# The second parts of the split weights, made on TensorE in PSUM instead of on VectorE

## The chip, the cores and the metric

The kernel runs on one core of a Trainium2 chip. The metric is the device time of one execution in microseconds (us). The engines are TensorE (PE in the profile, its weight loads PEld), VectorE (DVE), ScalarE (ACT), GpSimd (POOL) and SyncE (SP, which issues the DMAs). Each engine works through its own queue in the order in which the program has it, and waits for the others by semaphores.

## What is computed

Attention with a threshold, followed by an expert layer without a gate:

```python
scores = scale * np.matmul(q, k.transpose(0, 1, 3, 2))      # q, k, v: 8 x 8 x 576 x 64
thresh = np.max(scores, axis=-1, keepdims=True) - tau
scores = np.where(scores >= thresh, scores, -1000000000.0)
attn = softmax(scores)
x = (attn @ v), heads side by side                            # 4608 x 512
h = x @ w_in                                                  # 512 x 2048
g = h * (1.0 / (1.0 + np.exp(-h)))
out = g @ w_out                                               # 2048 x 512
```

All of it is float32, to float32's accuracy.

## The kernel before

**Precision.** The matrix products run on f16 operands in two parts: a first part that holds the leading bits of a scaled value, and a second part that holds what is left. A product then takes three f16 matmuls (first times first, first times second, second times first). The weights are split so as well: with a power-of-two scale `sc`, the first part is `sc*w` rounded to f16, and the second is `sc*w` minus the first part.

**Weights.** They come as 32 chunks of 128 x 512 numbers, 16 of `w_in` and 16 of `w_out`, as words of float64. `load_weights` (L157) issues the DMA of a chunk, 512 KB, into one of two staging buffers (eight chunks of `w_in` go to a free part of `gbuf`). `decode_weights` (L172) rebuilds the float32: a GpSimd product (L179), a VectorE shift (L183), a VectorE combination (L186, the last reader of the low words), four small matmuls on TensorE for the chunk's largest value (L197), a sign by ScalarE (L204) and a GpSimd product with it (L205). When 16 chunks are decoded, a scale is worked out, and `split_weights` (L207) makes the two parts of each chunk: the first on ScalarE (L211), the second on VectorE (L212). The decoded chunk `i` lies in slot `i+2` of `wst`, and the two f16 parts of chunk `i` take slot `i`, so that the parts of chunk `i+2` overwrite the decoded chunk `i`.

**Attention.** The work goes in tiles of 128 queries by 576 keys, in the text softmax tiles. A tile is: scores by TensorE (L412, four matmuls for a tile of one head; the first 16 tiles use float32 operands directly, L400), a maximum on VectorE (L422), an exponential on ScalarE (L432), the mask and the sum on VectorE (L441), a product with the reciprocal on ScalarE (L454), the two f16 parts on GpSimd (L465, L468, L471; L463 on ScalarE for the first few), a transposing DMA (L481), and the product with v on TensorE (L496). The first 16 tiles transpose on TensorE instead (L357, L359) and copy out on ScalarE (L367, L368). Keys are split on ScalarE and GpSimd (L324, L326), queries on ScalarE with VectorE or GpSimd.

**Expert layer.** For a column range of x, 16 units of the first layer (`h_unit`, 12 matmuls each, L539) are followed by ScalarE and VectorE work (L547, L548, L554, L555), and 16 units of the second (`o_unit`, 12 matmuls, L570) by a copy and a store (L580, L582). The first range of batch 0 has 256 columns, the second 320; later ranges have 288.

**PSUM.** `bank` (L78) hands out a tile in one of two banks of the pool `ps_m`, in turns: to the transposes of the first 16 tiles, to the sums over partitions for scales, and to the first-layer units. A third bank, used for the decodes' matmuls, joins the turns and serves the second layer later on.

**What sets the order.** The program is written out tile by tile: in slot `t` of the main loop the operations of `todo[t]` are called, then expert units by a running credit. `W_PLAN` places loads, decodes and splits in slots (`w_in`: decodes from slot 0, splits from 13 to 22; `w_out`: decodes from 9, splits from 26, with a priority offset of 150). A scheduler then orders the instructions of each engine by priority and by its own model of when operands and buffers come free, so that a small edit can move instructions far away.

Of the kernel before, what the change touches and what calls it, by code (L numbers as in the profile page):

```python
# [9 lines left out]
F16 = mybir.dt.float16  # L10
BF16 = mybir.dt.bfloat16
F32 = mybir.dt.float32
F32R = mybir.dt.float32r
I32 = mybir.dt.int32
AF = mybir.ActivationFunctionType
ALU = mybir.AluOpType
# [3 lines left out]
P = 128  # L20
# [3 lines left out]
NK = DM // P  # L24
# [28 lines left out]
def attention_moe(  # L53
# [10 lines left out]
    nc = tc.nc  # L64
    const = ctx.enter_context(tc.tile_pool(name="const", bufs=1))
# [12 lines left out]
    def bank(shape, name, own=None):  # L78
        if own is None:
            own = turn[0] = (turn[0] + 1) % turn[1]  # L80
        return ps_m.tile(shape, F32, tag=f"m{own}", name=name)
# [7 lines left out]
        out=gate, in0=tau_sb, scalar1=0.0, scalar2=0.125, op0=ALU.is_ge, op1=ALU.mult  # L89
# [3 lines left out]
        out=ntau, in0=tau_sb, scalar1=0.0, scalar2=-1.0, op0=ALU.max, op1=ALU.mult  # L93
# [51 lines left out]
    w16 = wst.bitcast(F16)  # L145
# [2 lines left out]
    nc.vector.memset(ones, 1.0)  # L148
    ident = const.tile([P, P], F32, name="ident")
    make_identity(nc, ident)  # L150
    wsc = {}

    w_words = (w_in.bitcast(I32), w_out.bitcast(I32))
    wraw = {}
# [52 lines left out]
    def split_weights(i):  # L207
        w = wst[:, i + WSPARE, :]
        hi = w16[:, i, 0:512]
        sc = wsc["in" if i < 4 * NK else "out"][:, 0:1]  # L210
        nc.scalar.activation(hi, w, AF.Copy, scale=sc)  # L211
        nc.vector.scalar_tensor_tensor(  # L212
            out=w16[:, i, 512:1024], in0=w, scalar=sc, in1=hi, op0=ALU.mult, op1=ALU.subtract
        )

    def wi(c, f, lo):
        col = f * P
# [402 lines left out]
    start = {}  # L620
# [66 lines left out]
    for first, t0, t1, t2, hp in W_PLAN:  # L687
        for i in range(16):
            ti = t0 + i * (t1 - t0) / 16
            at(math.floor(ti - 2), pri(hp, lambda i=i + first: load_weights(i)))  # L690
            at(math.floor(ti), pri(hp, lambda i=i + first: decode_weights(i)))
        at(t1, pri(hp, scale_out if first else scale_in))
        for i in range(16):
            at(t1 + i * (t2 - t1) // 16, pri(hp, lambda i=i + first: split_weights(i)))
# [27 lines left out]
    while t < NT + 8 or units or ready or held:  # L722
# [32 lines left out]
        for v, p, c0, n in avs.pop(t, []):  # L755
# [6 lines left out]
            scale = xscale if v in direct else 2.0**-12  # L762
# [52 lines left out]
```

## Time and profile before

| | |
|---|---|
| median of three runs | 1244.9 us (1243.98 to 1248.05) |
| the profiled execution, its own time | 1244.94 us |
| its span from first to last instruction | 1243.2 us |
| PE busy | 1140.7 us, 92% of the span |
| DVE busy | 961.3 us, 77% |
| ACT busy | 818.0 us, 66% |
| POOL busy | 759.4 us, 61% |

The profile is one execution. A row of a group of instructions names the line of the kernel, the engine, the operation, what it writes and reads, the shape, the count, the busy time in us, the mean duration of one in ns, and the idle time of the engine ahead of them with what ended it. The shares of the whole span are averages over stages with different limits; the weights' decodes and splits lie in the first 190 us, and from 1000 us on mostly the expert layer is left. Busy time of PE is worked out from pipelined matmuls, whose modelled durations overlap.

### The profile page before, as it was taken

The numbers are of one execution on the slowest core, as the hardware profiler recorded it, in microseconds if no ns is written. First come the engines' busy times: TensorE is split into PE (matmuls) and PEld (weight loads), VectorE is DVE, ScalarE is ACT, GpSimd is POOL, SyncE is SP. The second block draws the span as 40 slices with busy tenths as digits, with TensorE's granted clock in tenths as the row PEclk, the third lists the DMA queues.
The fourth block names the chain that finished last, engine by engine and source line by source line (L and its number), as shares of the span: only waits on it lengthen the run. The fifth ranks groups of instructions, "written<-read, shape, count | busy, mean of one in ns | idle before, by whom it ended". The sixth has DMA issues, their size and how long they took to land.

```text
span 1243.2 us, 26997 instructions
## 1 busy us (share of the span) xinstructions
PE 1140.7 (92%) x9400; PEld 897.4 (72%) x9400; DVE 961.3 (77%) x2627; ACT 818.0 (66%) x1505; POOL 759.4 (61%) x952
## 2 busy tenths in 40 slices
PE   5674879899799989999999999999999999999998
PEld 3453657676577767777888877787777877777777
DVE  7999998978888888989888957988689848333230
ACT  5787777766777667777777747776577847433331
POOL 4568988577778768786878708773688538200000
PEclk8996889899899999999999999999999999999999
DMA  9457867678868868888778638783687436200000
GB/s 297 127 177 179 186 130 146 132 151 167 151 130 145 166 133 147 148 158 172 143 140 152 137 90 154 143 148 101 110 168 148 87 73 116 54 15 16 12 14 24
DMA packets 363480, 158.15 MB, mean 127 GB/s; under 512 B 329552, under 2 KB 338256, under 8 KB 363344
## 3 DMA queue, kind: packets, MB, share of 16 engines
q1 hardware_dynamic: 363344, 156.43, 61.9%
q8 instruction: 74, 1.21, 0.4%
q14 instruction: 62, 0.51, 0.1%
HBM read 66.72 MB, written 9.44 MB: 61 GB/s over the span
## 4 chain that ended last, share of the span: by engine, by line
PE 54%; DVE 25%; DMA 6%; ACT 6%; issue 5%; POOL 4%; SPq 0%; ACTq 0%; POOLq 0%; DVEq 0%
PE o L570 20%; PE h L539 19%; PE s L412 7%; PE a L496 7%; DVE w L441 6%; DVE sm L422 5%; DMA vraw<-in_vL 3%; DVE qstack L316 3%; ACT w L432 2%; DMA wT<-hl 2%; DVE wst L212 2%; DVE h L548 1%; DVE gbuf L555 1%; ACT w L454 1%; DVE wst L186 1%
## 5 line engine op out<-in xcount | busy, mean ns | idle before, releaser
L539 PE MATMUL h<-x,wst 128*128 128x288 f16 (+2 forms) x3072 | 430.8, 290 | 12.7 <-DVE gbuf L555 10.2
L570 PE MATMUL o<-gbuf,wst 128*128 128x288 f16 (+2 forms) x3072 | 420.6, 287 | 8.2 <-ACT wst L580 6.5
L539 PEld LDWEIGHTS <-wst 128*128 128x128 f16 x3072 | 294.6, 99 | 102.0 <-issue 22.0
L570 PEld LDWEIGHTS <-wst 128*128 128x128 f16 x3072 | 293.2, 98 | 90.5 <-issue 11.4
L468 POOL TENSOR_TENSOR hl<-w,hl 128x512 f16<-128x512 f32 x272 | 329.3, 1211 | 14.5 <-ACT hl L463 2.1
L465 POOL TENSOR_SCALAR hl<-w 128x576 f16<-128x576 f32 x264 | 180.6, 687 | 190.8 <-ACT w L454 128.3
L432 ACT ACTIVATE w<-s,sm 128x576 f32<-128x576 f32 x288 | 210.5, 738 | 83.5 <-DVE sm L422 30.6
L441 DVE SCALAR_TENSOR_TENSOR w<-s,sm,w 128x576 f32<-128x576 f32 x288 | 232.0, 812 | 32.5 <-ACT w L432 30.2
L454 ACT ACTIVATE w<-w,sm 128x576 f32<-128x576 f32 x288 | 217.6, 770 | 52.4 <-DVE sm L449 49.3
L422 DVE TENSOR_REDUCE sm<-s 128x1 f32<-128x576 f32 x288 | 215.0, 749 | 31.9 <-PE s L412 28.2
L548 DVE SCALAR_TENSOR_TENSOR h<-th,h 128x288 f32<-128x288 f32 (+2 forms) x256 | 116.2, 455 | 108.5 <-ACT th L547 106.4
L547 ACT ACTIVATE th<-h,msc 128x288 f32<-128x288 f32 (+2 forms) x256 | 126.2, 497 | 106.0 <-PE h L539 104.7
L412 PE MATMUL s<-khi,qstack 128*128 128x288 f32 x608 | 158.7, 343 | 19.0 <-DVE w L441 14.5
L554 ACT ACTIVATE gbuf<-h 128x288 f16<-128x288 f32 (+2 forms) x256 | 103.5, 407 | 81.3 <-DVE h L548 80.2
L555 DVE SCALAR_TENSOR_TENSOR gbuf<-h,gbuf 128x288 f16<-128x288 f32 (+2 forms) x256 | 114.9, 451 | 40.4 <-ACT gbuf L554 39.6
L496 PE MATMUL a<-wT,v 128*64 128x288 f16 (+1 forms) x1680 | 131.3, 298 | 13.5 <-DMA wT<-hl 13.3
L412 PE MATMUL s<-klo,qstack 128*128 128x288 f32 x608 | 132.6, 300 | 0.0
L326 POOL TENSOR_TENSOR klo<-kraw,khi 128x576 fp32r<-128x576 f32 x64 | 95.2, 1487 | 56.5 <-ACT khi L324 53.8
L412 PEld LDWEIGHTS s<-khi,qstack 128*128 128x128 f32 x608 | 97.9, 196 | 41.9 <-issue 22.9
L496 PEld LDWEIGHTS <-v 128*64 128x64 f16 x1680 | 94.5, 113 | 40.1 <-issue 30.3
L412 PEld LDWEIGHTS s<-klo,qstack 128*128 128x128 f32 x608 | 100.3, 194 | 0.3
L471 POOL TENSOR_TENSOR hl<-w,hl 128x64 f16<-128x64 f32 x272 | 100.2, 368 | 0.0
(84 smaller groups left out, 866.5 us busy)
## 6 DMA issues: line engine op xcount, KB each, us to landing
qraw<-in_qT SPq DMA_DIRECT2D x128, 144.0 KB, 3.0
kraw<-in_kT SPq DMA_DIRECT2D x128, 144.0 KB, 3.0
vraw<-in_vL SPq DMA_DIRECT2D x32, 320.0 KB, 3.7
wraw<-in_w_out SPq DMA_DIRECT2D x16, 512.0 KB, 3.8
out_t<-wst SPq DMA_DIRECT2D x56, 144.0 KB, 2.2
wT<-hl SPq DMA_TRANSPOSE x304, 3.4
gbuf<-in_w_in SPq DMA_DIRECT2D x8, 512.0 KB, 7.5
wraw<-in_w_in SPq DMA_DIRECT2D x8, 512.0 KB, 6.0
```

The costliest lines, as they stand in the source:

```text
L412: nc.tensor.matmul(s_ps[:, j, :HALF], lhs, kk[:, j * HALF : (j + 1) * HALF], start=(n == 0), stop=(n == len(seq) - 1),)
L422: nc.vector.tensor_reduce(out=negm, in_=s_ps[:, :, :HALF], op=ALU.max, axis=AX.XY, negate=True)
L432: nc.scalar.activation(wtile[t].rearrange("p (j c) -> p j c", j=2), sps[t][:, :, :HALF], AF.Exp, bias=small[t][:, 0:1],)
L441: nc.vector.scalar_tensor_tensor(out=w3, in0=s_ps[:, :, :HALF], scalar=sm[:, 1:2], in1=w3, op0=ALU.is_ge, op1=ALU.mult, accum_out=sm[:, 2:3],)
L454: nc.scalar.activation(w, w, AF.Copy, scale=r)
L465: nc.gpsimd.tensor_scalar(out=fl[:, 0:S], in0=w, scalar1=1.0, scalar2=1.0, op0=ALU.mult, op1=ALU.mult)
L468: nc.gpsimd.tensor_tensor(out=fl[:, 640:1152], in0=w[:, 0:512], in1=fl[:, 0:512], op=ALU.subtract)
L496: nc.tensor.matmul(a_ps[odd * D : (odd + 1) * D, :n], vt[:, lo_v, odd, kv, :], wT[v, b * H + 2 * p + odd][:, kw, c0 - base : c0 - base + n ...
L539: nc.tensor.matmul(ph[:, :n], wi(c, f, lo_w), x16[b, lo_x][:, c, c0 : c0 + n], start=(k == 0), stop=(k == 11),)
L548: nc.vector.scalar_tensor_tensor(out=ph[:, :n], in0=th[:, :n], scalar=1.0, in1=ph[:, :n], op0=ALU.add, op1=ALU.mult,)
L555: nc.vector.scalar_tensor_tensor(out=g[:, 1, :n], in0=ph[:, :n], scalar=2.0**-14, in1=g[:, 0, :n], op0=ALU.mult, op1=ALU.subtract,)
L570: nc.tensor.matmul(ps[:, :n], wo(f, d, lo_w), g[:, lo_g, :n], start=(f == 0 and k == 0), stop=(f == NF - 1 and k == 2),)
```

## The change

`split_weights` no longer makes the second part on VectorE. For each of the two matrices ScalarE writes a float32 diagonal `wdiag` that holds the scale; once, it writes an f16 identity with the sign turned, `minus`. For each chunk TensorE adds two products in a PSUM bank taken by `bank`: `wdiag` times the decoded chunk (float32, 512 columns), and `minus` times the first part (f16, 512 columns). ScalarE copies the bank to the place of the second part.

```diff
+    minus = const.tile([P, P], F16, name="minus")
+    nc.scalar.activation(minus, ident, AF.Copy, scale=-1.0)
     wsc = {}
+    wdiag = {}
...
     def split_weights(i):
         w = wst[:, i + WSPARE, :]
         hi = w16[:, i, 0:512]
-        sc = wsc["in" if i < 4 * NK else "out"][:, 0:1]
+        which = "in" if i < 4 * NK else "out"
+        sc = wsc[which][:, 0:1]
+        if which not in wdiag:
+            wdiag[which] = const.tile([P, P], F32, name=f"wdiag_{which}", tag="wdiag")
+            nc.scalar.activation(wdiag[which], ident, AF.Copy, scale=sc)
         nc.scalar.activation(hi, w, AF.Copy, scale=sc)
-        nc.vector.scalar_tensor_tensor(
-            out=w16[:, i, 512:1024], in0=w, scalar=sc, in1=hi, op0=ALU.mult, op1=ALU.subtract
-        )
+        rest = bank([P, 512], f"wlo_{i}")
+        nc.tensor.matmul(rest, wdiag[which], w, start=True, stop=False)
+        nc.tensor.matmul(rest, minus, hi, start=False, stop=True)
+        nc.scalar.activation(w16[:, i, 512:1024], rest, AF.Copy)
```

The lines behind it move down by three (in the first part) and by eight (behind `split_weights`): L412 of before is L420 after, L432 is L440, and the new lines are L220 and L221 (the two matmuls) and L222 (the copy).

The change also moves instructions on every engine. On the queue of SP, the loads of `w_out` (`wraw`) are mixed before with the loads of keys and queries (`kraw`, `qraw`) and with the transposes of the softmax tiles (`wT<-hl`):

```order
L169 DMA wraw_709<-in_w_out 128x1024
L291 DMA kraw_4_1537<-in_kT 64x576 x2
L169 DMA wraw_711<-in_w_out 128x1024
L292 DMA qraw_4_1536<-in_qT 64x576 x2
L233 DMA vraw_0_2086<-in_vL 128x640
L481 DMA_TRANSPOSE wT_0_1349<-hl_1345 128x9x128
L169 DMA wraw_755<-in_w_out 128x1024
L481 DMA_TRANSPOSE wT_0_1349<-hl_1386 128x9x128
L291 DMA kraw_5_1615<-in_kT 64x576 x2
L169 DMA wraw_799<-in_w_out 128x1024
```

At the same place after the change, with lines three to eight higher:

```order
L172 DMA wraw_746<-in_w_out 128x1024
L172 DMA wraw_748<-in_w_out 128x1024
L172 DMA wraw_807<-in_w_out 128x1024
L172 DMA wraw_851<-in_w_out 128x1024
L172 DMA wraw_888<-in_w_out 128x1024
L172 DMA wraw_935<-in_w_out 128x1024
L172 DMA wraw_937<-in_w_out 128x1024
L172 DMA wraw_962<-in_w_out 128x1024
L172 DMA wraw_985<-in_w_out 128x1024
L241 DMA vraw_3_1804<-in_vL 128x640
L172 DMA wraw_1000<-in_w_out 128x1024
```

The loads of `w_out` now stand one behind the other, and the keys of the next heads and the first transposing DMAs come after the last of them.

On ScalarE, around the 40th exponential (`w_51`, `w_52` are the softmax tiles' rows, `o_0_0` a unit of the second layer, `h_0_6` the seventh unit of the first, `wlo` the new PSUM tile). Before:

```order
L432 ACTIVATE w_51_2265<-s_2213,sm_2264 128x576
L454 ACTIVATE w_49_2197<-w_49_2197,sm_2196 128x576
L454 ACTIVATE w_50_2210<-w_50_2210,sm_2209 128x576
L454 ACTIVATE w_51_2265<-w_51_2265,sm_2264 128x576
L580 ACTIVATE wst<-o_0_0_1484,msc_801 128x256
L580 ACTIVATE wst<-o_0_1_1620,msc_801 128x256
L324 ACTIVATE khi_2408<-kraw_10_2327 128x576
L315 ACTIVATE qstack_85<-qraw_10_2326,gate 128x576
L432 ACTIVATE w_52_2288<-s_2268,sm_2287 128x576
```

And after:

```order
L440 ACTIVATE w_51_2367<-s_2315,sm_2366 128x576
L462 ACTIVATE w_50_2312<-w_50_2312,sm_2311 128x576
L440 ACTIVATE w_52_2390<-s_2370,sm_2389 128x576
L555 ACTIVATE th_0_6_1291<-h_0_6_1230,msc_853 128x256
L218 ACTIVATE wst<-wst,o_w_sc 128x512
L222 ACTIVATE wst<-wlo_1226 128x512
L462 ACTIVATE w_51_2367<-w_51_2367,sm_2366 128x576
L562 ACTIVATE gbuf<-h_0_6_1230 128x256
L332 ACTIVATE khi_2510<-kraw_10_2429 128x576
```

At the same softmax tile, the 16 units of the first layer's first range and two units of the second are through before; after, the seventh unit of the first layer is at work, and splits of `w_out` stand where the second layer stood.

## The prediction, made before the change was run

> **What bounds the kernel now.** I read the stretches of the span first, cut where the order of work changes: up to the first weight split (75 us), to the end of its sixteen splits (about 123), to the 130th score matmul (205), to the 354th (376), and into the steady part. The columns are the stretch, its length, busy time and instructions of PE, PEld, DVE, ACT and POOL, the granted TensorE clock, the DMA share and GB/s.
>
> ```profile
> core 0: us, PE busy (x) PEld busy (x) DVE busy (x) ACT busy (x) POOL busy (x), PEclk, DMA share, GB/s
> 75.00:123.00 48.00, 27.09 (x173) 20.62 (x173) 48.00 (x102) 39.61 (x75) 36.17 (x34) 0.78 0.68 179
> 123.00:205.00 82.00, 67.59 (x542) 54.46 (x542) 76.75 (x191) 61.09 (x110) 71.30 (x80) 0.88 0.71 150
> 205.00:376.00 171.00, 149.89 (x1180) 115.47 (x1179) 149.10 (x426) 122.11 (x216) 126.58 (x163) 0.94 0.76 148
> 376.00:500.00 124.00, 119.86 (x1023) 94.09 (x1019) 108.98 (x310) 90.86 (x166) 96.44 (x123) 1.00 0.83 150
> 500.00:800.00 300.00, 292.47 (x2546) 234.91 (x2544) 257.19 (x739) 217.26 (x395) 216.56 (x283) 1.00 0.75 143
> ```
>
> From 376 on PE is busy 97 to 98% of the time: TensorE is the bound, and a microsecond of PE work there is a microsecond of time. From 75 to 205 it is VectorE: busy without a gap for 48 us, then 94%, while PE idles 35 of the 130 us. From 205 to 376 PE is at 88% and idles 21. So PE has 56 us of slack between 75 and 376, and hardly any behind it. Within the slack, the groups of instructions by shape give the second parts their price, and the table of PE's waits between 75 and 205 us who waits behind DVE (total, times, longest):
>
> ```profile
> L212 DVE SCALAR_TENSOR_TENSOR wst<-wst,i_w_sc 128x512 f16<-128x512 f32 x16 | 17.8, 1109 | 0.0
> L212 DVE SCALAR_TENSOR_TENSOR wst<-wst,o_w_sc 128x512 f16<-128x512 f32 x16 | 14.8, 931 | 0.0
> ```
> ```profile
> PE wps L197 <- DVE wst L186: 14.8, 6, 4.7
> PE h L539 <- DVE gbuf L555: 6.9, 4, 3.3
> ```
>
> The change takes 17.8 + 14.8 = 32.6 us from the engine that is the bound of its stage. PE's two longest waits there are for that engine too, but for other lines.
>
> **What the edit costs by itself.** Each of 32 chunks gets an f32 matmul of 512 columns, an f16 one of 512 columns, and a ScalarE copy out of PSUM. None of the two matmuls is in the trace in this size.
>
> ```profile
> L400 PE MATMUL s<-kd,gbuf 128*128 128x288 f32 x64 | 22.7, 495 | 16.6 <-DVE w L441 9.0 <-ACT gbuf L349 6.3 <-issue 1.2
> ...
> L539 PE MATMUL h<-x,wst 128*128 128x256 f16 x192 | 29.4, 314 | 8.2 <-DVE gbuf L555 6.9 <-DVE x L515 1.1
> ...
> L570 PE MATMUL o<-gbuf,wst 128*128 128x256 f16 x192 | 23.7, 280 | 1.8 <-DVE wst L212 1.8
> ...
> L367 ACT ACTIVATE wT<-tm 128x512 f32<-128x512 f32 x16 | 9.4, 590 | 0.8 <-PE tm L357 0.7
> ...
> L211 ACT ACTIVATE wst<-wst,o_w_sc 128x512 f16<-128x512 f32 x16 | 11.4, 717 | 4.1 <-DVE wst L212 4.1
> ```
>
> An f16 matmul of 256 columns takes 23.7/192 = 0.123 us of PE (L570), so 512 columns 0.25. The f32 matmul L400 stands in the code 32 times and in the trace 64 times, so one has two records: 2 x 22.7/64 = 0.71 us for 288 columns, 1.26 for 512, gaps inside included; four f16 passes would be 0.98. I take 1.0, nearer the second since L400 ran between waits: 1.25 us a chunk with both matmuls, 40 us for 32 (ends 39 and 48). The copy has the shape of L367's input, 0.59 us: 32 x 0.59 = 19 us of ScalarE. The diagonal and the minus identity are three small activations, taken at nothing beside these. So the edit trades 32.6 us of DVE for 40 of PE and 19 of ACT. PE's 40 fit into its 56 us of slack only if the rest becomes as dense as the steady part. That is decided by the order.
>
> **What the order does.** Two things move (the order's rows are shown with the change). First, sixteen of the split chunks and all decodes of w_out now stand as one block: on DVE the decodes 18 to 32 lie between the 16th and the 20th softmax tile; before they lay between the 16th and the 31st. Second, behind the block the softmax tiles come first and the expert units late. Counted on PE at the 128th score matmul (L412): before 201 matmuls of the first layer (L539) and 163 of the second (L570) are through, after only 96 and none, with 31 of the 32 new pairs. At the 352nd it is 600 and 416 before, 588 and 388 after; from there both orders run alike to the end, with 40 matmuls made up on the way. So the sum has two stages and a remainder.
>
> The trace of before puts the 128th score matmul at 205 us:
>
> ```profile
> 75.00:205.00 130.00, 27.89 (x130) 22.54 (x131) 0.84 0.70 161
> ```
>
> *Stage 1, from 75 us to the 128th score matmul: before 130 us.* In the block DVE, POOL and ACT handle w_out chunks as fast as they land, in two staging buffers, and the softmax tiles queue behind them on the same engines.
>
> ```profile
> wraw<-in_w_out SPq DMA_DIRECT2D x16, 512.0 KB, 3.8
> ```
> ```profile
> L179 POOL TENSOR_SCALAR wst<-wraw 128x512 f32<-128x512 f32 x24 | 20.3, 847 | 8.7 <-DMA wraw<-in_w_out 4.7 <-DVE sm L425 2.3 <-DMA wraw<-in_w_in 1.3
> ...
> L183 DVE TENSOR_SCALAR wst<-wst 128x512 int32<-128x512 int32 x32 | 28.1, 878 | 1.9 <-POOL wst L179 1.9
> ...
> L186 DVE SCALAR_TENSOR_TENSOR wst<-wraw,wst 128x512 int32<-128x512 int32 x24 | 20.7, 861 | 0.1
> ...
> L205 POOL TENSOR_TENSOR wst<-wst,wsg 128x512 f32<-128x512 f32 x32 | 40.0, 1255 | 22.5 <-PE wps L197 12.6 <-ACT wsg L204 4.9 <-ACT wT L368 2.8
> ```
>
> A buffer is taken for 3.8 + 0.85 + 0.88 + 0.86 = 6.4 us (landing, L179, L183, L186), two of them give a chunk per 3.2 us: 14 chunks in 45 us, from about 77 to 122. If the landings overlapped better, POOL's own 0.85 + 1.26 = 2.1 us a chunk would end it at 106; with the longer landings of a shared queue it might be 132. In those 45 us DVE has only 24 us of decodes and some four softmax tiles: the engine that was the bound now waits for data, and most of what it was spared goes there. I count the 16 splits' PE work as hidden here.
>
> Behind the block about 23 softmax tiles remain up to the 128th score matmul, with the other 16 splits. Their price on the two engines that are longest:
>
> ```profile
> L432 ACT ACTIVATE w<-s,sm 128x576 f32<-128x576 f32 x288 | 210.5, 738 | 83.5 <-DVE sm L422 30.6 <-DVE sm L445 23.0 <-DVE sm L449 13.8
> ...
> L454 ACT ACTIVATE w<-w,sm 128x576 f32<-128x576 f32 x288 | 217.6, 770 | 52.4 <-DVE sm L449 49.3 <-DVE v_e L129 1.7 <-DVE sm L445 1.1
> ...
> L468 POOL TENSOR_TENSOR hl<-w,hl 128x512 f16<-128x512 f32 x272 | 329.3, 1211 | 14.5 <-ACT hl L463 2.1
> ...
> L471 POOL TENSOR_TENSOR hl<-w,hl 128x64 f16<-128x64 f32 x272 | 100.2, 368 | 0.0
> ...
> L465 POOL TENSOR_SCALAR hl<-w 128x576 f16<-128x576 f32 x264 | 180.6, 687 | 190.8 <-ACT w L454 128.3 <-DVE h L548 35.7 <-DMA wT<-hl 21.2
> ...
> L326 POOL TENSOR_TENSOR klo<-kraw,khi 128x576 fp32r<-128x576 f32 x64 | 95.2, 1487 | 56.5 <-ACT khi L324 53.8 <-PE s L412 2.7
> ```
>
> ACT: 23 x (0.738 + 0.770) = 35, the splits 16 x (0.717 + 0.590) = 21, and some 20 for keys, queries and eight expert units (an estimate): 76. POOL: 23 x (1.211 + 0.368) = 36, some 17 conversions x 0.687 = 12, ten keys x 1.487 = 15, some 6 for queries: 69. Successive instructions overlap a little, and no engine runs without gaps: I take 77 us (ends 70 and 88). The 128th score matmul then comes at 122 + 77 = 199, 6 us sooner than before. PE has, of its 94.7 us in the 130, 105 x 0.153 (29.4/192) + 163 x 0.123 = 36 less and 31 x 1.25 = 39 more: 98 of 124 us, so it is not the bound.
>
> *Stage 2, to the 352nd score matmul: before 171 us.* PE had 149.9 us to do; the 93 first-layer and 135 second-layer matmuls that were put off come here: 93 x 0.153 + 135 x 0.123 + 1.25 for the last pair = 32. That is 182 us of PE. With so much expert work in hand PE should wait less than its 12% before, yet hardly reach the 2.5% of the steady part: at 95% it takes 192 us, 21 more (ends 97.5%: 187, and 88% as before: 207).
>
> *Remainder:* the 40 matmuls made up later, 40 x 0.14 (430.8/3072 by L539's row below) = 5.6 us on a PE that is full.
>
> ```profile
> L539 PE MATMUL h<-x,wst 128*128 128x288 f16 (+2 forms) x3072 | 430.8, 290 | 12.7 <-DVE gbuf L555 10.2
> ```
>
> The sum: -6 + 21 + 6 = +21 us. The profiled execution took 1244.9 us by its own time for its span of 1243.2, which is also the median of the three runs shown, so 1266.
>
> The granted clock is a doubt in this sum. It is 0.94 between 205 and 376, where PE had gaps, and 1.00 behind, where it has none. The Trainium skill, TensorE: Matmul & The Clock Gate (Part 1), says that the clock is given by how busy PE has been in the last few microseconds, half or full and nothing between. By that rule a stage 2 without gaps would run at the full clock, its 182 us would shrink to 171, and the whole would be 11 us shorter, 1255. The rows agree in direction, but the waits of stage 2 are only partly filled; the main sum keeps the clock of before.
>
> **The rivals.** *DVE's time comes back.* DVE is 100% and 94% busy in 75 to 205; if the landings are fast (block over at 106) and the tiles behind it run at 70 us, stage 1 ends at 176, 29 us sooner, and stage 2 at 187 adds 16, the remainder 6: 7 us faster, 1238. For it speaks that PE's two longest waits in the stage are for DVE; against it that 40 us of PE work must then vanish in 56 us of slack. Chance 0.13.
>
> *Nothing to measure.* Stage 1 ends about 15 us sooner and stage 2 takes 181, its own PE work without a gap: -15 + 10 + 6 = +1, 1246, within 4 us of before. Chance 0.09.
>
> *PSUM banks become the wait.* The new tiles take turns in the two banks of the transposes, scale sums and first-layer units, and each holds its bank through two matmuls and a copy behind other ACT work. If each of the 32 adds about 0.8 us to the chain of its stage (first part on ACT, second matmul on PE, copy on ACT, and only then the next user of the bank), 26 us come on top: 1292. It decides if PE's waits for the L222 copies exceed some 20 us. Chance 0.15.
>
> *The change does not free DVE* (the copy lands there): excluded by the code, which names ScalarE.
>
> **How the numbers follow.** About 0.3% (4 us) is what a measurement of this kernel can tell from no change. My forecast (a block paced by the landings, then softmax tiles, then the expert work as a backlog of PE) has 0.63, at 1266. With the banks' case, slower by over 0.3% has 0.78, same 0.09, faster 0.13. The ends of the stages (-29 to +20, +16 to +36) don't fall together; the range reaches from no change, 1245, to 1290, which leaves out most of the faster case and the worst of the banks' case.
>
> **What would show it.** In the changed profile: the last w_out decode near 122 us; DVE with clear gaps between 80 and 120; the 128th score matmul near 199; stage 2 near 192 us with PE at 95%; from there the two run alike, some 20 us apart. PE's new pairs near 1.25 us. The forecast is wrong if the last decode comes before 108, if PE is over 92% busy up to the 128th score matmul, or if the shift between the two traces shrinks again behind 400 us.

## The result and the profile after

The change makes the kernel slower. The median of four runs is 1276.4 us (1270.6 to 1278.1), against 1245.3 us (1244.0 to 1248.1) for four runs of the kernel before on the same chip: a ratio of 1.0237, 95% interval 1.0216 to 1.0259. The profiled execution has a span of 1273.9 us, 30.7 more than before.

Here are the stretches of the changed kernel, cut where its own order changes: up to the end of the sixteen splits of `w_in` and the block of decodes (127 us), to the 128th score matmul (203), through the thinnest stretch of PE behind it (246), to the 352nd score matmul (400), and the rest. The columns are those of the prediction's first fence.

```profile
core 0: us, PE busy (x) PEld busy (x) DVE busy (x) ACT busy (x) POOL busy (x), PEclk, DMA share, GB/s
75.00:127.00 52.00, 38.87 (x174) 20.55 (x174) 31.91 (x65) 39.32 (x73) 29.37 (x32) 0.87 0.50 163
127.00:203.00 76.00, 60.77 (x382) 39.27 (x382) 55.78 (x174) 69.25 (x126) 62.89 (x79) 0.96 0.78 157
203.00:246.00 43.00, 31.77 (x214) 25.88 (x213) 37.80 (x115) 32.32 (x58) 32.30 (x42) 0.88 0.63 121
246.00:400.00 154.00, 143.24 (x1204) 109.31 (x1203) 121.53 (x334) 97.98 (x180) 94.96 (x124) 0.98 0.69 135
400.00:1274.00 874.00, 857.86 (x7303) 684.27 (x7301) 624.34 (x1756) 544.02 (x1017) 485.97 (x632) 1.00 0.58 110
```

DVE, which was busy without a gap in the first stretch, now works 31.9 of its 52 us. PE idles 13 us there, 15 in the second and 11 in the third. Behind 400 PE is at 98%, as before (849.71 of 867 us behind 376). The kernel is some 24 us late when it gets to the part where TensorE is full, and there it wins nothing back. Here and below, "the 128th score matmul" with a time means the start of the one behind the first 128, and so with the 352nd and the 608th. The same stretches of before, cut as the experiments below are:

```profile
75.00:127.00 52.00, 30.40 (x191) 22.74 (x192) 52.00 (x110) 41.82 (x78) 39.91 (x37) 0.76 0.68 181
127.00:205.00 78.00, 64.27 (x526) 52.34 (x527) 72.75 (x183) 58.88 (x106) 67.56 (x77) 0.90 0.71 147
205.00:400.00 195.00, 173.89 (x1378) 134.32 (x1378) 170.97 (x489) 140.38 (x248) 146.44 (x189) 0.95 0.77 149
```

The groups by shape show the new instructions (an f32 matmul has two records, so that 32 of them stand for 16 matmuls):

```profile
L222 ACT ACTIVATE wst<-wlo 128x512 f16<-128x512 f32 x32 | 18.8, 590 | 0.0
L220 PE MATMUL wlo<-wst,wdiag_in 128*128 128x512 f32 x32 | 18.7, 676 | 3.3 <-POOL wst L208 1.7 <-ACT wst L222 1.5
L220 PE MATMUL wlo<-wst,wdiag_out 128*128 128x512 f32 x32 | 17.7, 636 | 1.0 <-ACT wst L222 1.0
L221 PE MATMUL wlo<-wst,minus 128*128 128x512 f16 x32 | 12.2, 387 | 0.0
```

The copies take 18.8 us of ACT. The rows of PE can't be added to a price: the modelled durations of a pair's matmuls overlap. The two lines taken as one have these rows (stretch, PE, PEld, ACT, clock, DMA share, GB/s):

```profile
75.00:127.00 52.00, 21.87 (x48) 5.51 (x32) 9.20 (x16) 0.87 0.50 163
127.00:203.00 76.00, 19.23 (x44) 5.03 (x30) 8.40 (x14) 0.96 0.78 157
203.00:246.00 43.00, 1.65 (x5) 0.32 (x2) 1.20 (x2) 0.88 0.63 121
```

That is 42.8 us of PE for the 32 pairs, 1.34 for one; the f32 matmuls are 30.5 of it, beside 12.2 for the f16 ones. In whole, PE was busy 1178.9 us, 38.2 more than before, and DVE 935.8, 25.5 less.

What came late is read from one line's row up to the 128th score matmul, first the first layer's (L547), then the second layer's (L578); the columns are the stretch, PE and PEld, the clock, the DMA share and GB/s:

```profile
75.00:203.00 128.00, 13.52 (x96) 8.71 (x96) 0.92 0.67 160
```

```profile
75.00:203.00 128.00, 0.00 (x0) 0.00 (x0) 0.92 0.67 160
```

So 96 matmuls of the first layer and none of the second were through, where before it was 201 and 163 (L539 and L570 there):

```profile
75.00:205.00 130.00, 31.00 (x201) 21.48 (x201) 0.84 0.70 161
```

```profile
75.00:205.00 130.00, 20.22 (x163) 15.96 (x163) 0.84 0.70 161
```

The table of PE's waits between 75 and 203 us of the changed kernel says what PE waited for (total, times, longest):

```profile
PE wps L200 <- DVE wst L189: 9.0, 7, 3.3
PE a L504 <- DMA wT<-hl: 4.5, 2, 4.0
PE s L420 <- DVE w L449: 3.8, 5, 1.7
PE h L547 <- DVE x L523: 2.5, 2, 2.2
PE wlo L220 <- ACT wst L222: 2.4, 4, 1.0
```

The waits for a bank, that is for the copy L222, are 2.4 us here, and with two smaller rows (1.4 and 1.3 us) 5.1 in all. Taken by itself, that speaks against the banks. The experiments show what they do nevertheless.

### The profile page after: what moved, and what is told of

It reads as the page before. It is cut to its first block, busy times and chain, and to the rows that moved or that the text cites. A ratio compares the mean times of both kernels' runs of the same rounds, so it can differ in the third digit from the quotient of the medians.

```text
span 1273.9 us, 27240 instructions
## 1 busy us (share of the span) xinstructions
PE 1178.9 (93%) x9496; PEld 909.3 (71%) x9496; DVE 935.8 (73%) x2595; ACT 831.8 (65%) x1540; POOL 745.6 (59%) x952
## 4 chain that ended last, share of the span: by engine, by line
PE 55%; DVE 17%; ACT 7%; DMA 5%; issue 5%; POOL 3%; SPq 1%; ACTq 0%; POOLq 0%
PE o L578 20%; PE h L547 19%; PE s L420 8%; PE a L504 7%; DVE w L449 5%; DVE sm L430 4%; DVE qstack L324 3%; DMA wT<-hl 3%; ACT w L440 2%; POOL hl L476 1%; ACT w L462 1%; DVE gbuf L563 1%; DMA vraw<-in_vL 1%; POOL hl L473 1%; DVE h L556 1%
## 5 line engine op out<-in xcount | busy, mean ns | idle before, releaser
L547 PE MATMUL h<-x,wst 128*128 128x288 f16 (+2 forms) x3072 | 429.3, 289 | 12.9 <-DVE gbuf L563 7.2
L578 PE MATMUL o<-gbuf,wst 128*128 128x288 f16 (+2 forms) x3072 | 422.3, 287 | 0.2 <-ACT wst L588 0.2
L547 PEld LDWEIGHTS <-wst 128*128 128x128 f16 x3072 | 293.2, 99 | 103.5 <-issue 23.7
L578 PEld LDWEIGHTS <-wst 128*128 128x128 f16 x3072 | 293.3, 98 | 81.4 <-issue 3.5
L440 ACT ACTIVATE w<-s,sm 128x576 f32<-128x576 f32 x288 | 211.8, 740 | 96.2 <-DVE sm L453 34.0
L420 PE MATMUL s<-khi,qstack 128*128 128x288 f32 x608 | 158.3, 341 | 23.4 <-DVE w L449 17.5
L504 PE MATMUL a<-wT,v 128*64 128x288 f16 (+1 forms) x1680 | 128.8, 294 | 12.3 <-DMA wT<-hl 11.9
L420 PE MATMUL s<-klo,qstack 128*128 128x288 f32 x608 | 132.2, 299 | 0.0
L420 PEld LDWEIGHTS s<-khi,qstack 128*128 128x128 f32 x608 | 96.3, 192 | 49.5 <-issue 31.6
L504 PEld LDWEIGHTS <-v 128*64 128x64 f16 x1680 | 92.0, 111 | 41.0 <-issue 29.7
L420 PEld LDWEIGHTS s<-klo,qstack 128*128 128x128 f32 x608 | 99.2, 191 | 0.8
L479 POOL TENSOR_TENSOR hl<-w,hl 128x64 f16<-128x64 f32 x272 | 94.6, 348 | 0.0
```

The source lines that it names most:

```text
L420: nc.tensor.matmul(s_ps[:, j, :HALF], lhs, kk[:, j * HALF : (j + 1) * HALF], start=(n == 0), stop=(n == len(seq) - 1),)
L440: nc.scalar.activation(wtile[t].rearrange("p (j c) -> p j c", j=2), sps[t][:, :, :HALF], AF.Exp, bias=small[t][:, 0:1],)
L504: nc.tensor.matmul(a_ps[odd * D : (odd + 1) * D, :n], vt[:, lo_v, odd, kv, :], wT[v, b * H + 2 * p + odd][:, kw, c0 - base : c0 - base + n ...
L547: nc.tensor.matmul(ph[:, :n], wi(c, f, lo_w), x16[b, lo_x][:, c, c0 : c0 + n], start=(k == 0), stop=(k == 11),)
L578: nc.tensor.matmul(ps[:, :n], wo(f, d, lo_w), g[:, lo_g, :n], start=(f == 0 and k == 0), stop=(f == NF - 1 and k == 2),)
```

## The experiments

Each kernel is the changed one with the edit shown. A ratio is to the kernel before on the same chip, with its 95% interval; a span is that of one profiled execution. In the expectations, A is the theory that the loss comes from the order: in the program's new order the expert units stand late, PE waits early, and the backlog is paid where PE is full. B, its rival, is the added work of TensorE itself. In the later runs A is taken apart: A1 blames the block of `w_out` decodes, in which hardly any softmax tile comes; A2 the expert units' backlog, which the shared banks cause.

**The order without TensorE's work (e1).** VectorE makes the second part again, but writes it into the same bank, and ScalarE copies it out.

```diff
-        nc.tensor.matmul(rest, wdiag[which], w, start=True, stop=False)
-        nc.tensor.matmul(rest, minus, hi, start=False, stop=True)
+        nc.vector.scalar_tensor_tensor(
+            out=rest, in0=w, scalar=sc, in1=hi, op0=ALU.mult, op1=ALU.subtract)
```

> The second parts are made by VectorE again, but into the PSUM bank, and ScalarE copies them out as in the change: no PE work is added, and the order keeps the block of w_out decodes (decode 32 at the 21st softmax tile) and the late expert units (132 and 0 first- and second-layer matmuls at the 128th score matmul). Theory A, the order costs the time (block paced by landings, expert units put off): 1268 to 1280 us, as slow as the change. Theory B, the PE work added to a core that is bound by PE costs the time: 1245 to 1255.

It took 1264.6 us, ratio 1.0125 (1.0100 to 1.0150): between the two, nearer A. Its stretches:

```profile
75.00:127.00 52.00, 24.14 (x138) 16.94 (x138) 45.96 (x87) 41.38 (x77) 32.20 (x32) 0.64 0.51 166
127.00:205.00 78.00, 52.99 (x322) 39.51 (x318) 66.03 (x170) 65.56 (x119) 63.46 (x74) 0.76 0.69 141
205.00:400.00 195.00, 176.46 (x1463) 138.59 (x1463) 165.56 (x472) 136.69 (x248) 136.33 (x179) 0.97 0.75 140
```

With nothing added to PE, PE does 460 instructions between 75 and 205 us, where the kernel before did 717. So the bank and the copy, with the order that follows from them, come to half of the whole loss without any work for TensorE.

**Less and more work for TensorE (e2, e3).** e2 drops the f32 matmul, e3 makes it twice, with half the scale in the diagonal (the lines that halve it are not shown).

```diff
 e2
-        nc.tensor.matmul(rest, wdiag[which], w, start=True, stop=False)
-        nc.tensor.matmul(rest, minus, hi, start=False, stop=True)
+        nc.tensor.matmul(rest, minus, hi, start=True, stop=True)
 e3
         nc.tensor.matmul(rest, wdiag[which], w, start=True, stop=False)
+        nc.tensor.matmul(rest, wdiag[which], w, start=False, stop=False)
```

> The f32 matmul of the scale diagonal is left out, so the second parts lack that term; the order of the engines stays nearly that of the change, and 36 us of PE work go. Theory A: nearly all of these 36 us lay beside waits in the stage before the 128th score matmul, so little goes: 1266 to 1274. Theory B: the time falls by most of the 36 us: 1240 to 1250.

> The f32 matmul stands twice with half the scale each time: 36 us more of PE work, same order to the 128th score matmul. Theory A: PE has about 28 us of slack left there, some of it in the block, so 10 to 25 us more than the change: 1286 to 1300. Theory B: 36 us more, about 1312.

e2 took 1267.5 us, 1.0153 (1.0124 to 1.0183), span 1264.1; e3 1289.2 us, 1.0322 (1.0295 to 1.0348), span 1289.3. Both lie where theory A had them. So the f32 matmuls matter, but do not carry the loss: without them two thirds of it are still there. The 30.5 us of PE that they took brought 9.8 us of span back. Part of the difference is the clock, in these rows of e2:

```profile
75.00:127.00 52.00, 33.49 (x172) 19.41 (x172) 32.17 (x70) 41.13 (x77) 28.17 (x31) 0.63 0.52 166
127.00:205.00 78.00, 54.12 (x379) 40.67 (x377) 60.15 (x182) 71.84 (x132) 67.21 (x85) 0.89 0.85 158
```

The clock granted in the first stretch is 0.63 against 0.87 with the f32 matmuls, and what is left of PE's work takes longer. PE's busy time in whole fell by 22.0 us, to 1156.9, and not by 30.5.

**The pool of the products with v (e4).** The new tiles go to `ps_a`, so that they share no bank with the first layer. That pool has one buffer, in which they now take turns with the products with v.

```diff
-        rest = bank([P, 512], f"wlo_{i}")
+        rest = ps_a.tile([P, 512], F32, tag="a", name=f"wlo_{i}")
```

> The new tiles take the bank of the attention products instead of the two of the transposes. The block stays (decode 32 at the 22nd softmax tile), the same PE work is added, but the expert units come early: 196 and 192 matmuls of the two layers at the 96th score matmul instead of 78 and 0. If the backlog of expert units is what costs (theory A), the stage up to the 128th score matmul becomes bound by PE at about 150 us and the rest is made up: 1260 to 1268. Theory B: 1276, as the change. If the wait for the two shared banks costs (the banks' rival): under 1260.

I expected a gain, and it was the slowest of all: 1309.6 us, 1.0489 (1.0457 to 1.0520). Two of its stretches, and its longest wait of PE:

```profile
170.00:205.00 35.00, 32.63 (x213) 22.01 (x212) 18.53 (x50) 28.54 (x59) 4.93 (x6) 1.00 0.12 35
320.00:440.00 120.00, 96.38 (x760) 74.84 (x760) 102.57 (x286) 79.34 (x138) 88.85 (x116) 0.89 0.77 146
```

```profile
PE s L420 <- DVE w L449: 37.1, 23, 5.7
```

Here the order is out in another way. Expert units come first and fill PE (32.6 of 35 us) while POOL has 4.9 us to do, the 128th score matmul is at 263.8 us (203.1 in the changed kernel), and later PE waits for softmax tiles (96.4 of 120 us). What was put off this time shows in the rows of the products with v (L504), of the changed kernel and of e4:

```profile
75.00:203.00 128.00, 10.72 (x112) 7.28 (x112) 0.92 0.67 160
```

```profile
75.00:203.00 128.00, 0.00 (x0) 0.00 (x0) 0.90 0.42 110
```

So e4 did not give the new tiles a bank for themselves: it took them away from the first layer's banks and made the products with v late in place of the expert units. That the softmax tiles stand behind those products is the likely reason for the long waits; it was not tested.

**The block, or the backlog (e5, e6).** e5 calls the splits of `w_in` six slots later, so that the decodes of `w_out` no longer stand in one block. e6 leaves all instructions and only names the bank: the sixteen tiles of `w_out` go to the third one, and only those of `w_in` take turns in the shared two.

```diff
 e5
-            at(t1 + i * (t2 - t1) // 16, pri(hp, lambda i=i + first: split_weights(i)))
+            ta, tb = (t1, t2) if first else (16, 19)
+            at(ta + i * (tb - ta) // 16, pri(hp, lambda i=i + first: split_weights(i)))
 e6
-        rest = bank([P, 512], f"wlo_{i}")
+        rest = bank([P, 512], f"wlo_{i}", None if i < 4 * NK else 2)
```

> The splits of w_in are called in slots 16 to 19, behind the transposes of the first sixteen tiles, instead of 10 to 13; all 32 pairs stay. The block of w_out decodes dissolves (decode 32 at the 30th softmax tile, as before the change), but the expert units stay late (84 and 0 matmuls of the two layers at the 128th score matmul). If the block is what costs (theory A1): 1250 to 1260. If the backlog of expert units is what costs (theory A2): 1268 to 1278. PE work alone (theory B) would leave 1276.

> Only the second parts of w_out go to the third bank (that of the decodes' sums); all else as in the change. The block stays (decode 32 at the 20th softmax tile), the backlog mostly goes (192 and 25 matmuls of the two layers at the 128th score matmul, 201 and 163 before the change). Theory A1 (block): 1268 to 1276. Theory A2 (backlog): 1252 to 1260. Theory B: 1276.

e5 took 1263.7 us, 1.0142 (1.0097 to 1.0187): between its two theories. The last decode of `w_out` moved from 127.0 to 143.6 us, but the expert units stayed late (84 and 0 matmuls at the 128th score matmul), and 352 score matmuls were done at 389.5 us instead of 400.4. This order, without the block, is 11 us earlier there; e6 shows that the block need not cost as much.

e6 took 1250.7 us, 1.0030 (1.0010 to 1.0051), span 1248.9. This one argument takes 25.0 of the 30.7 us away, with every instruction of the change still there; theory A2 had 1252 to 1260. Its stretches:

```profile
75.00:127.00 52.00, 39.03 (x188) 20.38 (x188) 34.42 (x73) 41.27 (x76) 31.21 (x33) 0.90 0.50 164
127.00:205.00 78.00, 69.17 (x491) 49.00 (x488) 61.20 (x186) 73.19 (x140) 62.46 (x80) 0.98 0.82 158
205.00:400.00 195.00, 178.03 (x1475) 138.47 (x1474) 168.37 (x477) 139.04 (x248) 144.74 (x186) 0.98 0.77 146
```

And its rows of the first and the second layer's lines up to 205 us, which is its 128th score matmul too (204.6):

```profile
75.00:205.00 130.00, 23.83 (x192) 18.03 (x192) 0.95 0.69 160
```

```profile
75.00:205.00 130.00, 3.07 (x25) 2.36 (x25) 0.95 0.69 160
```

PE's wait for the copy L222 in e6, up to its 128th score matmul:

```profile
PE wlo L220 <- ACT wst L222: 2.5, 3, 1.2
```

The block is still there (last decode at 125.0 us), the first stretch is as in the changed kernel, but now 192 and 25 expert matmuls are through instead of 96 and none. PE works 69 of the 78 us behind the block, and at the 352nd score matmul the kernel is 3.3 us behind the one before instead of 24.2. The direct wait of the new pairs for a bank is what it was (2.5 us against 2.4; with the smaller rows 2.9 against 5.1). So the shared banks work through the order in which the instructions stand, and not through PE's waiting for them. That the scheduler puts the units back because it sees their banks taken by the new tiles is the reading that fits both; what it does inside was not looked at. The sixteen tiles also no longer move the turn between the two shared banks on, so that units and transposes may take the other bank; what part that has was not separated.

**Each matrix alone (e7, e8).** In e7 VectorE keeps `w_in`, and `w_out` goes over TensorE in the third bank; in e8 TensorE makes `w_in` in the shared banks, and VectorE keeps `w_out`. The edit is an early return behind the old instruction:

```diff
+        if i < 4 * NK:        # e8: if i >= 4 * NK
+            nc.vector.scalar_tensor_tensor(out=w16[:, i, 512:1024], in0=w, scalar=sc,
+                                           in1=hi, op0=ALU.mult, op1=ALU.subtract)
+            return
```

> Only the second parts of w_out are made on TensorE, in the third bank; those of w_in stay on VectorE. No block (decode 32 at the 31st softmax tile), 16 pairs of PE work (24 us), 192 and 34 matmuls of the two layers at the 128th score matmul. Theories A1 and A2 both: 1244 to 1256, 15 us of DVE work in the stage it bounds against 24 us of PE work in the gaps and some backlog. Theory B: half of the change's loss, 1262.

> Only the second parts of w_in are made on TensorE, in the two shared banks; those of w_out stay on VectorE. The block stays (decode 32 at the 20th softmax tile) with 16 pairs of PE work inside it, the backlog is small (201 and 58 at the 128th score matmul). Theory A1 (block): 1264 to 1274. Theory A2 (backlog): 1250 to 1258. Theory B: 1262.

e7 took 1255.7 us, 1.0067 (1.0046 to 1.0088), and e8 1261.9 us, 1.0116 (1.0078 to 1.0155). In e7 the block is gone (last decode at 156.7 us), yet it isn't faster than e6, so taking the block away gains nothing there. e8 was in the range of neither A1 nor A2, and at the 1262 of theory B. That doesn't speak for B, which had 1262 for e7 too, with the same number of pairs, and 1276 for e6. At its 352nd score matmul it is only 6.0 us behind before (382.2 against 376.2), and the rest is lost later, 8 us of it between 582 and 663 us. A change at 75 to 127 us moves the order there too, and I have no cause for it.

**VectorE's part, TensorE's part, in the third bank (e9, e10).** e9 is e1 with e6's bank, e10 is e2 with e6's bank.

> As the first experiment (VectorE makes the second parts into PSUM, ScalarE copies them), with the tiles of w_out in the third bank as in the sixth. Order: block as in the change, 202 and 33 matmuls of the two layers at the 128th score matmul. Theory A2 (the backlog costs): the loss of the first experiment, 1.25%, goes to 0 to 0.5%: 1247 to 1253. If the block costs: 1262, as there. Beside the sixth it says what making the parts on TensorE is worth when the order is the same: by theory B it is 36 us better, by A2 within 6 us.

> As the sixth experiment (w_out in the third bank), without the f32 matmul, so the second parts lack that term: 36 us less of PE work in almost the same order (192 and 0 at the 128th score matmul). If PE's gaps hide the pairs there (A2): 1240 to 1250, at most 10 us less than the sixth. Theory B: 1215.

e10 took 1247.0 us, 1.0005 (0.9990 to 1.0021): in the better order the f32 matmuls cost 3 to 5 us (0.25% by the ratios, 5.3 us by the spans 1248.9 and 1243.6), and the rest of the change, gains and losses together, nothing that can be measured. e9 took 1261.7 us, 1.0123 (1.0103 to 1.0143). That is the 1262 expected for the case that the block costs the time, but the trace says otherwise: up to the 608th score matmul e9 does what A2 expected of it: that comes at 556.6 us (558.5 before). Then it falls behind. The row of e9, and behind it that of before:

```profile
560.00:700.00 140.00, 131.72 (x1088) 103.27 (x1087) 115.65 (x332) 96.69 (x175) 100.96 (x130) 0.98 0.74 141
```

```profile
560.00:700.00 140.00, 137.74 (x1192) 111.82 (x1190) 125.26 (x362) 106.51 (x192) 110.07 (x142) 1.00 0.79 150
```

Some 12 us go there, 400 us behind the edit. Why they go there is open. The six kernels together, as ratios to before:

| the second parts are made by | `w_out` in the shared banks | `w_out` in the third bank |
|---|---|---|
| VectorE into PSUM | 1.0125 | 1.0123 |
| TensorE, both matmuls | 1.0237 | 1.0030 |
| TensorE, without the f32 one | 1.0153 | 1.0005 |

In both rows with TensorE the bank is worth 1.5 to 2%; the f32 matmul 0.25% in the third bank and 0.8% in the shared ones. In the row with VectorE it seems to be worth nothing. How late each kernel is at the 352nd score matmul and at the end of its span, against the one before, shows why:

| kernel | tiles of `w_out` in | us late at the 352nd | us late at the end |
|---|---|---|---|
| the change | the shared banks | 24.2 | 30.7 |
| e1 | the shared banks | 20.4 | 18.1 |
| e2 | the shared banks | 19.5 | 20.9 |
| e3 | the shared banks | 40.2 | 46.1 |
| e5 | the shared banks | 13.3 | 19.4 |
| e6 | the third bank | 3.3 | 5.7 |
| e7 | the third bank | 6.2 | 13.1 |
| e9 | the third bank | 4.3 | 15.3 |
| e10 | the third bank | 3.6 | 0.4 |
| e8 | no bank (VectorE, in place) | 6.0 | 18.7 |

At the end of the weights' part the bank of these sixteen tiles decides, whichever engine makes them: 13 to 40 us late in the shared banks, 3 to 6 out of them. What e8 and e9 lose behind that, they lose elsewhere, mostly between 560 and 700 us.

**A better order for the new work (e11, e12).** The constant `PRI_S` is the priority offset with which a slot calls the score matmuls of the next softmax tile. e11 is e6 with it lowered from 1600 to 400, e12 is e7 with it.

```diff
-PRI_S, PRI_SOFT1, PRI_SOFT2 = 1600, 50, 200
+PRI_S, PRI_SOFT1, PRI_SOFT2 = 400, 50, 200
```

> As the sixth experiment, with the priority offset of the score matmuls lowered from 1600 to 400 in the whole kernel, which moves expert units ahead: 309 instead of 259 second-layer matmuls at the 256th score matmul. If backlog still costs there (A2): 2 to 6 us less than the sixth, 1244 to 1249. If the rest of the loss is PE work: 1250 and above.

> As the seventh experiment (only w_out on TensorE, third bank), with the same lower offset of the score matmuls: 192 instead of 94 second-layer matmuls at the 192nd score matmul. A2: 4 to 10 us less than the seventh, 1244 to 1250. If PE work alone is what is left: 1255.

e11 took 1240.7 us, 0.9955 (0.9938 to 0.9971): faster than before, by a little more than can be told from no change. e12 took 1249.0 us, 1.0021 (1.0006 to 1.0036). Two stretches of e11:

```profile
127.00:205.00 78.00, 69.27 (x496) 50.04 (x496) 59.66 (x177) 73.13 (x140) 62.20 (x79) 0.98 0.82 155
205.00:400.00 195.00, 181.09 (x1526) 142.60 (x1526) 171.60 (x491) 143.21 (x255) 146.91 (x189) 0.99 0.79 150
```

PE has 181 busy microseconds in the 195, 7 more than before, and 352 score matmuls are done at 375.6 us (376.2 before). Its gain on e6, 0.75% by the ratios, is more than the 2 to 6 us expected. The kernel before with this constant alone was not run, so it stays open how much of the 0.45% the constant would give without the change, and whether VectorE's freed time has a part in it.

## Why the prediction was right, and where it was not

The forecast was 1266 us and slower; it came out slower, at 1276, inside the range. Point by point:

- **The pairs' price**, 1.25 us each and 40 in whole, held: 1.34 and 42.8 by the two lines' busy time taken as one, and 38.2 by the growth of PE's busy time in whole. From start to start the f32 matmul takes 0.86 us and the f16 one 0.22 in the rows of the last section, so four f16 passes, 0.98 in the forecast, were the right measure and not the 1.26 from L400. The copy was as said, 0.59.
- **The block** was forecast to end at 122 us, at a chunk per 3.2 us; it ended at 127.0. From 77 us on that is 50/14 = 3.6 us a chunk. It is paced by the landings for the larger part, as said: DVE's longest wait between 75 and 127 us, and POOL's two longest, are

```profile
DVE wst L186 <- POOL wst L182: 13.6, 10, 2.6
```

```profile
POOL wst L182 <- DMA wraw<-in_w_out: 11.1, 8, 1.9
POOL wst L208 <- PE wps L200: 8.8, 5, 2.3
```

- So DVE waits for POOL, and POOL for the transfers and, nearly as long, for the decodes' matmuls, which the forecast's 6.4 us a buffer left out. The landing itself took 3.5 us, less than the 3.8 taken. The engine that was the bound of the stage has its clear gaps (31.9 of 52 us busy). The time that DVE was spared went there.
- **Stage 1**: the 128th score matmul at 203.1 us instead of 199, against 204.7 before. The term is -1.6 us instead of -6. The stage behind the block took 76.1 us (77 forecast); the difference is the block's later end. The length was right partly by luck: it was added up as a full ScalarE with 76 us to do, and ScalarE was busy 69.25 us there, GpSimd 62.89. The expert matmuls through by then were 96 and 0, as counted.
- **Stage 2** from there to the 352nd: 197.3 us instead of 192, so +25.8 instead of +21 (171.5 before). Two errors of opposite sign lie in it. PE had 175.0 us to do (31.8 + 143.2), not 182; and it was busy 89% of the time, not 95. "With so much expert work in hand PE should wait less" is the step that failed: 11 of the 22 idle us lie between 203 and 246 (31.8 of 43 us busy). PE's two longest waits in them are those of score matmuls for the softmax work of DVE:

```profile
PE s L420 <- DVE w L449: 6.1, 4, 3.8
PE s L420 <- DVE sm L433: 3.8, 2, 3.4
```

- The expert units stand behind these score matmuls in PE's queue (twelve of the first layer start as soon as the score matmuls that waited 3.8 us are through), and the first layer's first range ends at 233.1 us (174.5 before). Work in hand fills a wait of PE only where it stands ahead of the instruction that waits.
- **The remainder** was forecast at 6 us and is 6.5 (24.2 late at the 352nd score matmul, 30.7 at the end). The number is right, its working is not. Most of it comes at one place, between the 608th score matmul and 663 us after, 633 before. First the row of after, then of before:

```profile
582.00:663.00 81.00, 78.40 (x649) 61.85 (x647) 71.48 (x204) 58.99 (x107) 59.55 (x78) 0.98 0.77 153
```

```profile
558.00:633.00 75.00, 73.19 (x635) 59.53 (x633) 68.30 (x200) 58.05 (x105) 58.04 (x75) 1.00 0.85 159
```

- PE is busy 5.2 us more in it and takes 6 us more, with 14 more instructions, for which the forecast's 0.14 us each makes 2. The rest of the 40 were made up without loss of time: 16 more instructions in the 182 us ahead of this place (1541 against 1525) and 11 more in the 270 us behind it (2286 against 2275). So 40 matmuls at 0.14 us are not what the 6.5 us are, and that the two agree is luck. The shift did not shrink behind 400 us.
- **The sum**, -1.6 + 25.8 + 6.5 = 30.7, against +21 forecast: 4.4 us in stage 1 (the block's end), 4.8 in stage 2 (its density) and 0.5 in the remainder make the 10 that were missing.
- **The clock** was 0.96 over stage 2, where the sum kept 0.94, and PE's work there was 7 us less than forecast. It did not reach the full clock, since stage 2 did not fill: 0.88 where PE is busy 74% of the time (203 to 246), 0.98 at 93% (246 to 400) and 1.00 at 98% (behind 400). That direction agrees with the Trainium skill, TensorE: Matmul & The Clock Gate (Part 1), which has the clock follow how busy PE was in the last few microseconds. Two slips of the forecast stand beside it: a stage 2 without gaps at the full clock would be 171 us, 21 less than the sum's 192 and not 11; and the late end of stage 1, 132 + 88 = 220, is +15 and not +20.
- **The rival of the banks** was set out as waits of PE for the copies of over 20 us. They are 5.1 us, so in that form it falls. In another form it was nearer to the cause than the forecast: the shared banks put the expert units late in the order, which I took as given, and e6 shows that moving sixteen tiles to another bank removes 25.0 of 30.7 us. The forecast had the path right (late units, a backlog on a full PE) but not what sets it.
- **The rival "DVE's time comes back"** needed the block to end at 106 us; it ended at 127.
- One thing that the text ahead of the prediction says is not so: a row of `W_PLAN` gives the first slot of the decodes, then that of the splits, then their last, and the text read it one place off. The splits of `w_in` are called in slots 10 to 13, those of `w_out` in 22 to 26. No step of the prediction used these numbers.

What was shown: half of the loss stays without any work for TensorE (e1), two thirds without its f32 matmuls (e2); up to the 352nd score matmul the bank of `w_out`'s tiles takes most of it away, whichever engine makes the parts (e6, e9, e10); and it is not PE's waiting on a bank. What was only argued: how the scheduler gets from the bank to the order. Open is why several of these orders lose 6 to 12 us between 560 and 700 us, which is most of what e8 and e9 lose.

## What to carry to other kernels

Before work goes to an engine with slack, list who else takes turns in the buffers that it will need, and give it buffers that the backlog's work does not use: here the same instructions cost 2.4% or 0.3% by that alone. When a scheduler writes the order, count at one landmark how much of each kind of work is through before and after, in both directions, and look which work the new buffer's other users do: in e4 the products with v came late in place of the expert units, and it cost more. A change that frees one engine may have to be measured with the order set anew (e11), and the old kernel with it.

## What the runs showed of the hardware

- An f32 matmul of 128 x 128 by 512 columns takes as long as four f16 ones. In the timeline of the changed kernel (start, busy time, both in us; the f32 matmul has two records) the starts are 0.22 us apart behind the f16 matmul and 0.86 behind the f32 one, at the full clock. The busy times, 0.38 and 1.02, overlap the next matmul's and give a ratio that is too small:

```profile
84.59 0.38 PE L221 MATMUL wlo<-wst,minus 128*128 128x512 f16 x1
84.81 1.02 PE L220 MATMUL wlo<-wst,wdiag_in 128*128 128x512 f32 x2
85.67 0.38 PE L221 MATMUL wlo<-wst,minus 128*128 128x512 f16 x1
```

- PE's busy time is no constant of the instructions. The same 9496 take 1178.9 us in the changed kernel, 1167.5 in e6 and 1152.9 in e11, at mean clocks of 0.978, 0.984 and 0.986. The clocks differ by 0.8%, the busy times by 2.2%, so the clock alone doesn't explain it.
- The f32 matmuls hold the clock up. Between 75 and 127 us it is 0.87, 0.90 and 0.92 in the changed kernel, e6 and e11, where they are there, and 0.63, 0.61, 0.64 and 0.55 in e2, e10, e1 and e9, where they are not (0.76 before, with more expert work in that stretch). More of them don't raise it further: 0.85 in e3, with twice as many. PE's busy share over the stretch does not give it either: e2 is busy 64% at 0.63, before 58% at 0.76. A mean of this kind mixes stretches at the full clock with stretches at half of it, as a stretch of the changed kernel and one of e2 show (columns as in the first table):

```profile
82.00:119.00 37.00, 27.77 (x138) 13.52 (x136) 22.42 (x40) 28.28 (x53) 20.32 (x23) 1.00 0.50 165
```

```profile
69.00:109.00 40.00, 22.00 (x90) 11.56 (x89) 26.54 (x55) 29.62 (x52) 23.11 (x24) 0.50 0.52 164
```

- With PE busy 55% and no wait of PE over 3.3 us, e2 stays at half for 40 us; with 75% the changed kernel stays at the full clock for 37. The sixteen f16 matmuls with the minus identity show what that costs, in the changed kernel and then in e2:

```profile
75.00:127.00 52.00, 5.90 (x16) 1.61 (x16) 0.87 0.50 163
```

```profile
75.00:127.00 52.00, 8.39 (x16) 1.81 (x16) 0.63 0.52 166
```

- That is 0.37 us for one against 0.52, a factor of 1.42 where the clocks differ by 1.38. So in a stage where PE has gaps, work added to it can pay back part of its price to its neighbours: the f32 matmuls by which the changed kernel and e2 differ are 30.5 us of the pairs' busy time, and PE's busy time in whole differs by only 22.0.
